# Router logits of 14 token tiles by products in four column groups, closed one step later

## The chip, the cores and the metric

The kernel runs on one core of a Trainium2 chip. The metric is the time of one execution in microseconds (us) on the device; lower is better. Engines are called by the profile's short names: PE is TensorE's matrix products, PEld its weight loads, DVE is VectorE, ACT is ScalarE, POOL is GpSimd, SP is SyncE, which only issues transfers.

## What is computed

Three layers follow each other, all in float32, on 4 x 576 = 2304 tokens of 512 features:

```python
# 1. attention, 8 heads of 64, causal window of 64
scores = scale * np.matmul(q, k.transpose(0, 1, 3, 2))
attn = softmax(where(mask, scores, -1e9))
x = np.matmul(attn, v)                      # reshaped to 2304 x 512
# 2. noisy top-2 router over 8 experts, each 512 -> 1024 -> 512
logits = x @ w_gate
noise_scale = np.log1p(np.exp(x @ w_noise))
noisy_logits = logits + noise_scale * noise
top2 = np.argpartition(-noisy_logits, 2, axis=1)[:, :2]
out[mask] += top2_w[mask, k, None] * (relu(x[mask] @ w1[e]) @ w2[e])
# 3. a dense layer 512 -> 2048 -> 512 with a gated quadratic
h = x @ w_in
out = g(h) @ w_out
```

The change is in the two products `x @ w_gate` and `x @ w_noise`, which the kernel makes together: 16 columns per token, at full float32 precision, because a wrong choice of expert would show.

## The kernel before

The tokens are cut into 18 tiles of 128. The attention stage is a software pipeline of steps u = 0, 1, 2, ... (function `step`, L674); one tile takes two steps, here called a pair, and the order of instructions on every engine is exactly the order in which the code is written. A step issues, in this order:

- on even u: the scores of the next tile (`A`, a mask product L355 and then the key products L364, each in four 64x64 quadrants of PE), and the transposes of a finished attention tile (`Ex`, L421, copied out by ACT at L423);
- the transposes of the probabilities (`C`, L387, copied out by ACT at L389);
- on even u: the row maxima of the two new score blocks on DVE (`top`, L371), each turned into a bias by POOL (L373); then on every u the exponentials of one score block on ACT (`soft`, L380, four of 128 columns);
- on odd u: the router logits of an older tile (`logits`, which calls `Gm`);
- the next pieces of routing: `place` (products of one-hot marks on PE, L632), `early`, and `advance`, which runs some DVE instructions of the generator `route(g)` and up to 2 (later 4) pairs of marks, `ohr` on DVE (L584) and `ohe` on DVE (L591) or ACT (L594);
- on even u: probabilities times values (`Dm`, L401, in two column halves of PE, all into the two banks `OB`), its division on DVE (L406 to L409) and a store of the tile to DRAM;
- two halves of splitting an expert weight into a rounded part and a remainder, ACT first and DVE behind it (`split_w`, L161 and L162).

`Gm` (L434 to L442) multiplies the transposed tile, as the stationary operand, with the 512 x 16 gate matrix: four products over 128 rows each, accumulated into 16 columns (272 to 287) of a rotating bank, which DVE copies out (L442). A float32 product appears as two records in the trace.

```python
for k in range(4):
    nc.tensor.matmul(lg, lhsT=xt[:, k, :], rhs=wg_sb[:, k, 0:2 * E], start=(k == 0), stop=(k == 3))
```

The tiles are routed in three groups of six (`tile_group`); when the logits of a group's last tile are there, `route(g)` starts. When all marks of groups 0 and 1 are placed (24 products), `early` copies the result out (L459), works out the first token numbers of expert 0 (to L475) and POOL issues three gathers of those rows (L726). Their transposes (L748) start the expert stage; the last tiles of attention and routing are finished beside it (`tail`). The stages behind, the experts and the dense layer, keep PE at work to the end. Two banks, 3 and 5 (called bank_76 and bank_77 in the order below), rotate over `Ex`, `C`, `C` and `Gm` of every pair (`rot`).

Of the kernel before, what the change touches and what calls it, by code (L numbers as in the profile page):

```python
# [11 lines left out]
F32 = mybir.dt.float32  # L12
# [5 lines left out]
AF = mybir.ActivationFunctionType  # L18
ALU = mybir.AluOpType
AX = mybir.AxisListType  # L20

P = 128
# [4 lines left out]
E, F = 8, 1024  # L27
F2 = 2048
NT = N // P
# [8 lines left out]
GROUPS = [6, 6, 6]  # L38
EARLY = 2
NA = 3  # L40
MARKS, TAIL = (2, 4), 4
Y0, LOOK = 3, 1
PTB = 3
EW, L0, LS, F0 = 7, 1, 4, 1
SC, WS, HT = 10, 4, 256
G2 = [2, 4, 4, 4, 4]
# [12 lines left out]
def fused_kernel(ctx, tc, qT, kT, v, wg, noise, wcat, out, wd=None):  # L59
    nc = tc.nc  # L60
# [18 lines left out]
    wk = rte.enter_context(tc.tile_pool(name="wk", bufs=2, side="right"))  # L79
    gp = rte.enter_context(tc.tile_pool(name="gp", bufs=2, side="right"))  # L80
    oh = rte.enter_context(tc.tile_pool(name="oh", bufs=10, side="right"))
    ac = rte.enter_context(tc.tile_pool(name="ac", bufs=1, side="right"))
# [4 lines left out]
    OB = att.enter_context(tc.tile_pool(name="pso", bufs=1, space=PS)).tile([P, 2, 512], F32, name="ob")  # L87
# [14 lines left out]
    def load_qk(j):  # L102
        q_t[j] = qbuf[:, j % 2]
        kt = k_t[j] = qk.tile([P, 4, 320], F32, tag="k", name=f"k{j}")

        for h in (slice(0, P), slice(P, 256)) if j == 0 else (slice(0, 256),):
            t = slice(256 * j + h.start, 256 * j + h.stop)
            nc.sync.dma_start(out=kt[:, :, 64 + h.start:64 + h.stop], in_=kTv[:, :, t])
            nc.sync.dma_start(out=q_t[j][:, :, h], in_=qTv[:, :, t])
        if j == 0:  # L110
            nc.vector.memset(kt[:, :, 0:64], 0.0)


    def keys_before(j):
        nc.gpsimd.tensor_copy(k_t[j][:, :, 0:64], k_t[j - 1][:, :, 256:320])
# [4 lines left out]
    def load_v(i):  # L120
        a = vp.tile([P, H * VW], F32, tag="vE", name=f"vE{i}")
        nc.sync.dma_start(out=a, in_=v[P * i:P * i + P, :])
        if i == 0:
            vO[0] = vp.tile([P, H * VW], F32, tag="vE", name="vE_")
            nc.vector.memset(vO[0][64:128, :], 0.0)
            nc.sync.dma_start(out=vO[0][0:64, :], in_=v[0:64, :])
        vE[i] = a
# [6 lines left out]
    def load_raw(n, eng=nc.sync):  # L134
        if SP <= n < NCE:

            if n % 2 == 0:
                pool["pair"] = stream((n - SP) // 2, [P, 2, 1024], F32, f"w{n}")
            whi[n] = t = pool["pair"][:, n % 2, :]
        else:  # L140
            raws[n] = t = raw.tile([P, 1024], F32, tag="raw", name=f"raw{n}")
        if NF <= n < N2:

            if n % NF == 0:
                r = E - 2 if n >= NCE else (n // NF - 1) % (E - 2)
                dyn[n // NF] = nc.values_load(cnt_i[0:1, 1 + r:2 + r], engines=[mybir.EngineType.SP], min_val=0,
                                          max_val=(E - 1) * NF)
            eng.dma_start(out=t, in_=wcat[bass.ds(dyn[n // NF] + n % NF, 1)].rearrange("o p n -> (o p) n"))
        else:
            eng.dma_start(out=t, in_=wcat[n])  # L150
# [110 lines left out]
    wg_sb = ac.tile([P, 4, 32], F32, name="wg_sb")  # L261
# [12 lines left out]
    for s in (0, 64):  # L274
        nc.gpsimd.affine_select(out=id64[s:s + 64, :], in_=id64[s:s + 64, :], compare_op=ALU.not_equal, fill=1.0,
                                base=0, pattern=[[-1, 64]], channel_multiplier=1)
        m = m0[s:s + 64]
# [13 lines left out]
    idn = cst.tile([P, P], F32, name="idn")  # L291
# [39 lines left out]
    NU = 2 * NT  # L331
# [3 lines left out]
    LGO, POS, CNT = 272, 296, 320  # L335
    turn = [0]

    def rot(u):
        turn[0] += 1
        return bank[3 + 2 * (turn[0] % 2)] if u <= NU else bank[6]  # L340
# [3 lines left out]
    pr, pts, xts, xs, lgs_g, mxs = {}, {}, {}, {}, {}, {}  # L344


    def A(i):
        j = i // 2
        qo, ko = (i % 2) * P, (i % 2) * P
        sb = [Sb[(2 * i + k) % 3] for k in range(2)]  # L350
        for k in range(2):
            r = slice(64 * k, 64 * k + 64)
            for c in range(2):
                m = masks[c][int((2 * i + c) % 9 == 0)]
                nc.tensor.matmul(sb[k][64 * c:64 * c + 64, :], lhsT=id64[r, :],  # L355
                                 rhs=m[r].unsqueeze(1).to_broadcast([64, 4, P]), start=True, stop=False)
        for g in range(4):
            for c in range(2):
                for k in range(2):
                    r = slice(64 * k, 64 * k + 64)  # L360
                    keys = k_t[j][r, g, ko + 64 * c:ko + 64 * c + P]
                    if c == 0:
                        keys = keys.rearrange("p (s n) -> p s n", s=2)[:, ::-1, :]
                    nc.tensor.matmul(sb[k][64 * c:64 * c + 64, g * P:g * P + P],  # L364
                                     lhsT=q_t[j][r, g, qo + 64 * c:qo + 64 * c + 64],
                                     rhs=keys, start=False, stop=(g == 3))
# [16 lines left out]
    def C(u):  # L383
        p = pr.pop(u)
        PTb = rot(u)
        for g in range(4):
            nc.tensor.transpose(PTb[:, g * P:g * P + P], p[:, g, :], idn)  # L387
        t = wk.tile([P, 512], F32, tag="pt", name=f"pt{u}", bufs=PTB)
        nc.scalar.activation(t, PTb, AF.Copy)  # L389
        pts[u] = t  # L390
# [37 lines left out]
    tile_group = {}  # L428
# [2 lines left out]
            tile_group[s + t] = (g, t)  # L431


    def Gm(i, u):  # L434
        g, t = tile_group[i]
        xt = xts.pop(i)
        lg = (rot(u) if u <= NU else bank[0])[:, LGO:LGO + 2 * E]
        for k in range(4):
            nc.tensor.matmul(lg, lhsT=xt[:, k, :], rhs=wg_sb[:, k, 0:2 * E], start=(k == 0), stop=(k == 3))
        if t == 0:  # L440
            lgs_g[g] = gp.tile([P, max(GROUPS), 2 * E], F32, tag="lgs", name=f"lgs{g}", bufs=3)
        nc.vector.tensor_copy(lgs_g[g][:, t, :], lg)  # L442


    state = {"C": zero8, "late": False, "first": False}
# [6 lines left out]
    def finish_ids(parts, dst=True):  # L452


        if dst:
            f1 = wk.tile([P, 512], F32, tag="pt", name="f1", bufs=PTB)
            f2 = wk.tile([P, 512], F32, tag="pt", name="f2", bufs=PTB)
        else:
# [165 lines left out]
    live, rows = [], {}  # L624
# [39 lines left out]
        soft(u)  # L664
    warm(4)

    def logits(i, u):
        Gm(i, u)
        g, t = tile_group[i]
        if t == GROUPS[g] - 1:  # L670
            live.append(route(g))
            next(live[-1])

    def step(u):  # L674
        for c in range(EW):
            if u == L0 + LS * c:
                load_raw(c)
        if u + 2 < NU:
            if (u + 2) % 4 == 0 and (u + 2) // 4 + 1 < NT // 2:
                load_qk((u + 2) // 4 + 1)  # L680
                keys_before((u + 2) // 4 + 1)
            if (u + 1) % 2 == 0 and (u + 1) // 2 + 1 < NT:
                load_v((u + 1) // 2 + 1)


        m = u // 2
        if u % 2 == 0:
            if u + 2 < NU:
                A(m + 1)
            if 0 <= m - 2 < NT:  # L690
                Ex(m - 2, u)
        if u < NU:
            C(u)
        if u % 2 == 0 and u + 2 < NU:
            top(u + 2)
            top(u + 3)
        if u + 2 < NU:
            soft(u + 2)

        if u % 2 == 1 and 0 <= m - 2 < NT:  # L700
            logits(m - 2, u)
        place()
        early()
        advance(MARKS[u > NU - 10])
        if 0 <= u - 1 < NU:
            Dm(u - 1)

        for c in range(EW):
            for h in range(2):
                if u == L0 + LS * c + 3 + h:  # L710
                    split_w(c, h)
            if u == L0 + LS * c + 4 and EW <= c + 2 < NF:
                load_raw(c + 2)
# [56 lines left out]
    pool["w7"] = w7.enter_context(tc.tile_pool(name="w7", bufs=1, reuse_waits="tile"))  # L770

    def tail():
        logits(NT - 2, NU + 1)
        Ex(NT - 1, NU + 1)
        advance(TAIL)
        yield
        logits(NT - 1, NU + 1)
        while live or oq or pq:
            place()
            advance(TAIL)  # L780
            yield
        finish_ids([(NA, NB), (0, NA), (NB, E * JB)])
        prep_gather(units[1], 0)
        count()
        rte.close()
        pool["xp"] = xpc.enter_context(tc.tile_pool(name="xp", bufs=2, reuse_waits="tile", side="right"))
        for n in range(NF, NF + 2):
            load_raw(n)
        yield
        for b in range(1, units[1]["nb"]):  # L790
            prep_gather(units[1], b)
            yield
        prep_gather(units[2], 0)

    def count():
# [26 lines left out]
        for a, src in enumerate((src_i, dst_i)):  # L822
            f = wk.tile([P, 512], F32, tag="pt", name=f"rk{a}", bufs=PTB)[:, 0:R * J * E]
            f = f.rearrange("p (r j e) -> p r j e", j=J, e=E)
# [481 lines left out]
    for s in range(len(seq)):  # L1306
        ui, n = seq[s]
        un = units[ui]
        f = n - un["ch"][0]
# [112 lines left out]
    for q, (ui, p) in enumerate(items):  # L1422
# [5 lines left out]
        while ndone < len(items) and ndone <= q + (1 if items[ndone][0] == FIRST2 else 2):  # L1428
            i = items[ndone]
# [9 lines left out]
        g = gate(*items[q + 1]) if q + 1 < len(items) and items[q + 1][0] > FIRST2 else []  # L1439
# [58 lines left out]
```

## Time and profile before

| | |
|---|---|
| median of 3 runs | 969.06 us (968.68 to 971.01) |
| the profiled execution, its own time | 969.4 us |
| its span in the trace | 967.7 us |
| span of the attention stage, to the first transposes of gathered rows | 0 to 102.8 us |
| PE busy over the span | 98% |
| DVE, ACT, POOL busy over the span | 68%, 46%, 23% |

Busy shares are means over stages with different limits. PE's records are pipelined and their ends are modelled, so a busy PE can still have waited: the distance from the start of one group of products to the start of the next is the safer reading. Idle time is named in a row by "[us <-releaser]", and "issue" is a wait for nothing that the profile shows.

### The profile page before, as it was taken

How to read it: one execution, taken by the hardware profiler on the slowest of the kernel's cores; microseconds unless marked ns; L12 is line 12 of the kernel's file. 1: busy time of each engine (PE TensorE's matmuls, PEld its weight loads, DVE VectorE, ACT ScalarE, POOL GpSimd, SP SyncE). 2: the span in 40 equal slices, each digit the busy share in tenths (PEclk: the TensorE clock that was granted, in tenths of full speed). 3: DMA queues.
4: the chain of work that ended last, by engine and by line, in shares of the span. 5: the costliest groups of instructions: out<-in, count | busy, mean ns of one | idle time of the engine just before them, and what ended most of it. 6: DMA issues, size and time to landing. Idle time of an engine off the chain costs nothing. (4 is left out here: it accounts for less than half of the span.)

```text
span 967.7 us, 18329 instructions
## 1 busy us (share of the span) xinstructions
PE 944.2 (98%) x6918; PEld 837.0 (86%) x6918; DVE 660.7 (68%) x1377; ACT 446.8 (46%) x921; POOL 218.6 (23%) x269
## 2 busy tenths in 40 slices
PE   8998899999999999999999999999999999999997
PEld 6887789998898988889888888888999899899996
DVE  4689375578997968798442366666766777677664
ACT  6887224356555555555332366344325334442221
POOL 3221113244535434344301020013002201300000
PEclk9999799999999999999999999999999999999999
DMA  8875116557877976967837357584576558556521
GB/s 249 294 236 177 56 45 204 209 195 254 285 253 261 288 250 215 298 218 238 331 118 273 119 197 244 195 302 138 175 261 213 173 174 305 174 164 209 187 95 44
DMA packets 92797, 201.17 MB, mean 208 GB/s; under 512 B 7433, under 2 KB 17929, under 8 KB 92705
## 3 DMA queue, kind: packets, MB, share of 16 engines
q1 hardware_dynamic: 85264, 177.84, 55.4%
q0 software_dynamic: 6144, 19.76, 5.7%
q10 hardware_dynamic: 1296, 2.36, 0.6%
q8 instruction: 55, 0.90, 0.4%
q14 instruction: 38, 0.30, 0.1%
HBM read 159.65 MB, written 40.29 MB: 207 GB/s over the span
## 5 line engine op out<-in xcount | busy, mean ns | idle before, releaser
L935 PE MATMUL bank<-wo,hg 128*128 128x512 f32 x864 | 238.2, 394 | 0.0
L935 PE MATMUL bank<-w,he 128*128 128x512 f32 (+3 forms) x696 | 170.5, 396 | 0.0
L935 PEld LDWEIGHTS bank<-wo,hg 128*128 128x128 f32 x864 | 147.0, 189 | 17.3
L935 PEld LDWEIGHTS bank<-w,he 128*128 128x128 f32 (+3 forms) x696 | 124.7, 184 | 26.7
L869 PE MATMUL bank<-xhie,w 128*128 128x288 f32 (+4 forms) x768 | 120.9, 299 | 1.6 <-DVE he L880 1.5
L869 PEld LDWEIGHTS bank<-xhie,w 128*128 128x128 f32 x768 | 112.0, 188 | 8.6 <-DVE he L880 3.5
L877 ACT ACTIVATE he<-bank 128x288 fp32r<-128x288 f32 (+4 forms) x96 | 40.2, 419 | 149.7 <-PE bank L869 146.1
L162 DVE TENSOR_TENSOR w<-raw,w 128x1024 fp32r<-128x1024 f32 (+1 forms) x71 | 82.0, 1154 | 32.8 <-ACT w L161 32.1
L1188 PEld LDWEIGHTS bank<-xb,wi 128*128 128x128 f32 x576 | 81.6, 191 | 12.2 <-ACT r L887 1.7
L1188 PE MATMUL bank<-xb,wi 128*128 128x256 f32 x576 | 85.9, 285 | 2.4 <-ACT r L887 1.4
L1212 ACT ACTIVATE hg<-cg 128x512 fp32r<-128x512 f32 x64 | 40.3, 629 | 100.5 <-DVE cg L1210 100.5
L1188 PEld LDWEIGHTS bank<-xc,wi 128*128 128x128 f32 x480 | 67.2, 188 | 7.6 <-DVE wg L1173 0.6
L1048 POOL TENSOR_TENSOR y<-y,y 128x512 f32<-128x512 f32 x14 | 19.1, 1362 | 228.2 <-ACT y L1047 228.2
L1188 PE MATMUL bank<-xc,wi 128*128 128x256 f32 x480 | 70.2, 281 | 0.2
L161 ACT ACTIVATE w<-raw 128x1024 fp32r<-128x1024 f32 (+1 forms) x71 | 69.3, 977 | 0.0
L869 PE MATMUL bank<-xloe,w 128*128 128x288 f32 (+4 forms) x384 | 68.1, 299 | 0.0
L880 DVE SCALAR_TENSOR_TENSOR he<-bank,he 128x320 fp32r<-128x320 f32 (+8 forms) x120 | 43.2, 399 | 34.0 <-ACT he L877 33.9
L207 POOL TENSOR_TENSOR td<-rawd 128x512 f32<-128x512 f32 x32 | 33.3, 1040 | 133.5 <-DVE rawd L205 73.7
L1206 ACT ACTIVATE mg<-cg 128x512 f32<-128x512 f32 x64 | 40.0, 626 | 48.6 <-DVE cg L1178 46.9
L1207 DVE SCALAR_TENSOR_TENSOR cg<-mg,cg 128x512 f32<-128x512 f32 x64 | 46.9, 733 | 18.8 <-ACT mg L1206 18.8
L869 PEld LDWEIGHTS bank<-xloe,w 128*128 128x128 f32 x384 | 57.4, 188 | 0.0
L1216 DVE SCALAR_TENSOR_TENSOR hg<-cg,hg 128x512 fp32r<-128x512 f32 x64 | 45.9, 717 | 9.1 <-ACT hg L1212 8.7
(301 smaller groups left out, 1587.0 us busy)
## 6 DMA issues: line engine op xcount, KB each, us to landing
wi<-w1o SPq DMA_DIRECT2D x56, 1024.0 KB, 5.5
raw<-wcat SPq DMA_DIRECT2D x64, 512.0 KB, 5.5
rawd<-wd SPq DMA_DIRECT2D x32, 512.0 KB, 5.0
w1o<-so SPq DMA_DIRECT2D x64, 256.0 KB, 5.7
y<-y_dram SPq DMA_DIRECT2D x30, 256.0 KB, 5.4
vE<-v SPq DMA_DIRECT2D x18, 260.0 KB, 4.7
x_dram<-x SPq DMA_DIRECT2D x18, 256.0 KB, 2.3
k<-kT SPq DMA_DIRECT2D x8, 512.0 KB, 6.6
```

The source lines that it names most:

```text
L161: nc.scalar.activation(w[:, 0, c], t[:, c], AF.Copy)
L162: nc.vector.tensor_tensor(out=w[:, 1, c], in0=t[:, c], in1=w[:, 0, c].bitcast(F32), op=ALU.subtract)
L207: nc.gpsimd.tensor_tensor(out=t, in0=hf, in1=lf, op=ALU.add)
L869: nc.tensor.matmul(ps, lhsT=l[k], rhs=r[:, k, s:s + w], start=(c == 0), stop=(c == len(prods) - 1))
L877: nc.scalar.activation(hh, ps, AF.Relu)
L880: nc.vector.scalar_tensor_tensor(out=t, in0=ps[:, c], scalar=0.0, in1=hh[:, c].bitcast(F32), op0=ALU.max, op1=ALU.subtract)
L935: nc.tensor.matmul(M2[b][0:w], lhsT=h2[:, o:o + w], rhs=r[n], start=(first and a == 0), stop=(last and a == end))
L1188: nc.tensor.matmul(ps, lhsT=w[:, l, k * P:k * P + P], rhs=r[:, m, k, :], start=(c == 0), stop=(c == len(prods) - 1))
L1206: nc.scalar.activation(st["m"], c, AF.Relu, scale=0.5)
L1207: nc.vector.scalar_tensor_tensor(out=c, in0=st["m"], scalar=1.0, in1=c, op0=ALU.min, op1=ALU.subtract)
L1212: nc.scalar.activation(h2[:, 0:T], c, AF.Copy, scale=-1.0)
L1216: nc.vector.scalar_tensor_tensor(out=h2[:, T:2 * T], in0=c, scalar=-1.0, in1=h2[:, 0:T].bitcast(F32), op0=ALU.mult, op1=ALU.subtract)
```

## The change

For 14 tiles (0 to 14 without 11) the stationary and the moving operand of the logit products change places. `fold` makes four products with 32 columns of the gate matrix as the stationary operand and the transposed tile as the moving one. Each writes its own 32 partitions of a bank and takes its own 32 columns of PE; they are not accumulated. The result, four partial sums below each other, is copied to SBUF as `lt` (128 x 128), by DVE for tiles 0 to 6 and by ACT for the others. One step later, on even u between `C` and `Dm`, `unfold` makes one product of `lt` with `sel`, a 128 x 16 matrix that adds the four partial sums, into columns 272 to 287 of the second bank of `OB`, which the values leave free; DVE copies the 16 columns out (`keep_logits`). Tile 11, the last of group 1, and tiles 15 to 17 stay as they were.

```diff
+FOLD = 15
...
+    folded = {}
+    sel = ac.tile([P, 2 * E], F32, name="sel")
+    nc.gpsimd.tensor_tensor(out=sel, in0=idn[:, 0:2 * E], in1=idn[:, 32:32 + 2 * E], op=ALU.add)
+    for c in (64, 96):
+        nc.gpsimd.tensor_tensor(out=sel, in0=sel, in1=idn[:, c:c + 2 * E], op=ALU.add)
+
+    def fold(i, u):
+        xt, bk = xts.pop(i), rot(u)
+        for k in range(4):
+            nc.tensor.matmul(bk[32 * k:32 * k + 32, 0:P], lhsT=wg_sb[:, k, :], rhs=xt[:, k, :], start=True, stop=True)
+        lt = wk.tile([P, P], F32, tag="lt", name=f"lt{i}")
+        if i < FOLD // 2:
+            nc.vector.tensor_copy(lt, bk[:, 0:P])
+        else:
+            nc.scalar.activation(lt, bk[:, 0:P], AF.Copy)
+        folded[i] = lt
+
+    def unfold(i):
+        lg = OB[:, 1, LGO:LGO + 2 * E]
+        nc.tensor.matmul(lg, lhsT=folded.pop(i), rhs=sel, start=True, stop=True)
+        keep_logits(i, lg)
...
+    def direct(i):
+        return i >= FOLD or tile_group[i][0] == EARLY - 1 and tile_group[i][1] == GROUPS[EARLY - 1] - 1
...
         if u % 2 == 1 and 0 <= m - 2 < NT:
-            logits(m - 2, u)
+            (Gm if direct(m - 2) else fold)(m - 2, u)
+        if u % 2 == 0 and 0 <= m - 3 < NT and not direct(m - 3):
+            unfold(m - 3)
         place()
```

How it moves instructions is shown at three places. The first is PE at the end of the stage, at tile 14 (p are probabilities, x the attention tile, ohe and ohr marks). Before:

```order
L387 MATMUL bank_77<-idn,p_1826 128x128 x4
L439 MATMUL bank_76<-wg_sb,xt_1894 128x16 x4
L632 LDWEIGHTS ohr_2_0_1919
L632 MATMUL bank_78<-ohe_2_0_1921,ohr_2_0_1919 128x145
```

and the next step of the same program:

```order
L421 MATMUL bank_77<-idn,x_1954 128x128 x4
L387 MATMUL bank_76<-idn,p_1910 128x128 x4
L632 LDWEIGHTS ohr_4_0_1978
L632 MATMUL bank_78<-ohe_4_0_1980,ohr_4_0_1978 128x145
L632 LDWEIGHTS ohr_4_1_1982
```

With the change, the same two steps:

```order
L388 MATMUL bank_77<-idn,p_1866 128x128 x4
L444 MATMUL bank_76<-xt_1935,wg_sb 32x128 x4
L662 LDWEIGHTS ohr_2_0_1962
L662 MATMUL bank_78<-ohe_2_0_1964,ohr_2_0_1962 128x145
```

```order
L422 MATMUL bank_77<-idn,x_1997 128x128 x4
L388 MATMUL bank_76<-idn,p_1951 128x128 x4
L454 MATMUL ob<-sel,lt_2016 128x16
L662 LDWEIGHTS ohr_4_0_2022
L662 MATMUL bank_78<-ohe_4_0_2024,ohr_4_0_2022 128x145
L662 LDWEIGHTS ohr_4_1_2026
```

The four logit products keep their place in the odd step, in another shape, and one product (L454) comes in on the even step, ahead of the last products of marks.

The second place is DVE where the route of group 1 begins, with the logits of tile 11 (m, t, uu, w are the first results of the route; ohr_5 and ohe_5 are the last marks of group 0). Before:

```order
L591 TENSOR_SCALAR ohe_5_1_1571<-io_179,rf_1276 128x145
L406 TENSOR_SCALAR rl_1589<-ob 128x8
L407 RECIPROCAL rl_1589<-rl_1589 128x8
L409 TENSOR_TENSOR x_1592<-ob,rl_1589 128x512
L442 COPY lgs_1048<-bank_77 128x16
L500 TENSOR_SCALAR m_1616<-lgs_1048 128x48
L503 SCALAR_TENSOR_TENSOR t_1618<-m_1616,lgs_1048 128x48
L371 TENSOR_REDUCE mx_1656<-bank_73 128x4
```

With the change:

```order
L410 TENSOR_TENSOR x_1619<-ob,rl_1616 128x512
L461 COPY lgs_1124<-bank_77 128x16
L530 TENSOR_SCALAR m_1643<-lgs_1124 128x48
L614 TENSOR_SCALAR ohr_5_0_1645<-io_179,rf_1358,tcode_184 128x128
L621 TENSOR_SCALAR ohe_5_0_1647<-io_179,rf_1358 128x145
L533 SCALAR_TENSOR_TENSOR t_1649<-m_1643,lgs_1124 128x48
L614 TENSOR_SCALAR ohr_5_1_1655<-io_179,rf_1358,tcode_184 128x128
L621 TENSOR_SCALAR ohe_5_1_1657<-io_179,rf_1358 128x145
L372 TENSOR_REDUCE mx_1691<-bank_73 128x4
```

Group 0's logits are complete one step later, so its route runs one step later throughout, and its last two pairs of marks now stand inside group 1's route, behind its first instruction.

The third place is ACT at tile 10 (p are the exponentials, w a half of a weight to split, xt the transposed tile). Before:

```order
L380 ACTIVATE p_1490<-bank_73,nb_1436 128x128 x4
L594 ACTIVATE ohe_4_0_1504<-io_179,rf_1276 128x145
L594 ACTIVATE ohe_4_1_1508<-io_179,rf_1276 128x145
L161 ACTIVATE w_1477<-raw_1241,w_1477 128x512
L423 ACTIVATE xt_1542<-bank_76 128x512
```

With the change:

```order
L381 ACTIVATE p_1514<-bank_73,nb_1458 128x128 x4
L449 ACTIVATE lt_1523<-bank_77 128x128
L162 ACTIVATE w_1501<-raw_1259 128x512
L424 ACTIVATE xt_1567<-bank_76 128x512
L390 ACTIVATE pt_1573<-bank_77 128x512
L381 ACTIVATE p_1583<-bank_74,nb_1576 128x128 x4
L624 ACTIVATE ohe_4_0_1594<-io_179,rf_1358 128x145
```

The copy `lt` stands ahead of the weight's half, and the two marks of group 0 have gone to the step behind. SP issues the same transfers in the same order, and behind the attention stage no engine's order differs.

## Rows read from the trace of the kernel before

**Rows 1.** Windows of the trace: the attention stage in three parts, its end, the start of the experts.

```profile
core 0: us, PE busy (x) PEld busy (x) DVE busy (x) ACT busy (x) POOL busy (x), PEclk, DMA share, GB/s
20.00:60.00 40.00, 39.62 (x725) 35.51 (x727) 29.79 (x92) 35.66 (x104) 10.26 (x30) 1.00 0.80 266
60.00:80.00 20.00, 18.88 (x353) 16.21 (x353) 17.18 (x55) 16.93 (x51) 3.97 (x12) 1.00 0.79 257
80.00:99.20 19.20, 16.45 (x264) 14.23 (x260) 18.09 (x80) 14.12 (x41) 3.45 (x8) 1.00 0.32 108
99.20:111.40 12.20, 7.74 (x59) 7.04 (x60) 3.73 (x11) 2.30 (x5) 2.96 (x4) 0.58 0.35 109
111.40:125.00 13.60, 13.60 (x87) 12.63 (x85) 7.06 (x38) 3.61 (x8) 0.00 (x0) 1.00 0.00 0
```

**Rows 2.** Timeline of PE over two pairs; start us, us, engine, instruction.

```profile
44.12 0.96 PE L439 MATMUL bank<-wg_sb,xt 128*128 128x16 f32 x8
45.02 0.50 PE L355 MATMUL bank<-mask,id 64*64 64x512 bf16 x4
...
48.91 0.96 PE L439 MATMUL bank<-wg_sb,xt 128*128 128x16 f32 x8
49.81 0.41 PE L355 MATMUL bank<-mask,id 64*64 64x512 bf16 x4
50.05 1.04 PE L364 MATMUL bank<-k,qbuf 64*64 64x128 f32 x32
51.02 0.65 PE L421 MATMUL bank<-idn,x 128*128 128x128 f32 x4
...
53.62 0.96 PE L439 MATMUL bank<-wg_sb,xt 128*128 128x16 f32 x8
```

**Rows 3.** Waits between 20 and 62 us: who waited for what, us in total, times, longest.

```profile
PEld bank L421 <- issue: 1.4, 8, 0.2
PEld ob L401 <- issue: 1.3, 8, 0.2
```

**Rows 4.** Timeline of ACT, the same pairs and tile 10's marks; idle time in brackets.

```profile
43.92 1.14 ACT L380 ACTIVATE p<-bank,nb 128x128 f32<-128x128 f32 x4 [0.62 <-POOL nb L373]
...
50.97 0.71 ACT L161 ACTIVATE w<-raw 128x512 fp32r<-128x512 f32 x1
...
53.42 1.14 ACT L380 ACTIVATE p<-bank,nb 128x128 f32<-128x128 f32 x4 [0.62 <-POOL nb L373]
54.43 0.62 ACT L389 ACTIVATE pt<-bank 128x512 f32<-128x512 f32 x1
...
72.09 0.80 ACT L594 ACTIVATE ohe<-io,rf 128x145 f16<-128x145 f16 x2
```

**Rows 5.** Timeline of DVE over the same stretch.

```profile
50.28 0.17 DVE L442 COPY lgs<-bank 128x16 f32<-128x16 f32 x1
...
51.72 0.69 DVE L162 TENSOR_TENSOR w<-raw,w 128x512 fp32r<-128x512 f32 x1 [0.42 <-ACT w L161]
52.33 1.28 DVE L371 TENSOR_REDUCE mx<-bank 128x4 f32<-128x512 f32 x2
```

**Rows 6.** Timeline of DVE, group 0's marks, group 1's route and the first token numbers.

```profile
73.43 0.69 DVE L162 TENSOR_TENSOR w<-raw,w 128x512 fp32r<-128x512 f32 x1 [1.17 <-ACT w L161]
...
90.99 0.31 DVE L584 TENSOR_SCALAR ohr<-io,rf,tcode 128x128 f16<-128x128 f16 x1
91.22 0.26 DVE L591 TENSOR_SCALAR ohe<-io,rf 128x145 f16<-128x145 f16 x1
91.38 1.28 DVE L371 TENSOR_REDUCE mx<-bank 128x4 f32<-128x512 f32 x2
...
96.88 0.46 DVE L459 COPY first<-bank 128x290 f32<-128x290 f32 x1 [0.32 <-PE bank L632]
```

**Rows 7.** Timeline of POOL and PE, the first gather and the transposes of what it brings.

```profile
98.43 1.21 POOL L726 DMA_INDIRECT xg0a<-x_dram,src_i  x1 [4.84 <-DVE rl L406]
```
```profile
102.78 0.75 PE L748 MATMUL bank<-idr,xg0a 128*128 128x128 f32 x4 [3.46 <-DMA xg0a<-x_dram,src_i]
```

More of the change, by code (lines that the diff above doesn't have):

```diff
@@ L431, in fused_kernel, with keep_logits @@
             tile_group[s + t] = (g, t)
+    folded = {}
[17 more added lines that the diff above has]
+        keep_logits(i, lg)
+    def keep_logits(i, lg):
+        g, t = tile_group[i]
+        if t == 0:
+            lgs_g[g] = gp.tile([P, max(GROUPS), 2 * E], F32, tag="lgs", name=f"lgs{g}", bufs=3)
+        nc.vector.tensor_copy(lgs_g[g][:, t, :], lg)
+        if t == GROUPS[g] - 1:
+            live.append(route(g))
+            next(live[-1])
     def Gm(i, u):
@@ L439, in Gm @@
             nc.tensor.matmul(lg, lhsT=xt[:, k, :], rhs=wg_sb[:, k, 0:2 * E], start=(k == 0), stop=(k == 3))
-        if t == 0:
-            lgs_g[g] = gp.tile([P, max(GROUPS), 2 * E], F32, tag="lgs", name=f"lgs{g}", bufs=3)
-        nc.vector.tensor_copy(lgs_g[g][:, t, :], lg)
+        keep_logits(i, lg)
     state = {"C": zero8, "late": False, "first": False}
@@ L665, in fused_kernel @@
     warm(4)
[L667 to L672, printed above, removed]
+    def direct(i):
+        return i >= FOLD or tile_group[i][0] == EARLY - 1 and tile_group[i][1] == GROUPS[EARLY - 1] - 1
     def step(u):
@@ L772, in tail @@
     def tail():
-        logits(NT - 2, NU + 1)
+        Gm(NT - 2, NU + 1)
         Ex(NT - 1, NU + 1)
@@ L776, in tail @@
         yield
-        logits(NT - 1, NU + 1)
+        Gm(NT - 1, NU + 1)
         while live or oq or pq:
```

## The prediction

> **What bounds the kernel now.** Read the windows first [rows 1]. Behind 111.4 us PE has no free time (13.60 of 13.60 us), and the change moves nothing there. So the question is when the expert stage can start, and that is one event: the transposes of gathered rows start at 102.78 us, when the gather lands, after PE has waited 3.46 us for it [rows 7]. The gather was issued at 98.43 us, as soon as DVE had the first token numbers; DVE reads the placed marks out at 96.88 us, 0.32 us after it ran dry, waiting for the last product of marks [rows 6]. A microsecond that the attention stage gains or loses counts only where it reaches that read-out.
>
> Now go back along the stage and ask in each part which engine sets the pace. Between 20 and 60 us PE is busy 39.62 of 40 us, which looks like a PE bound [rows 1]. The timeline of PE says otherwise: pairs last 4.79 and 4.71 us in turn (44.12 to 48.91 to 53.62), and in the longer one the mask products last 0.50 us instead of 0.41 [rows 2]: their second bank waits 0.09 us for the exponentials of an earlier score block. Follow those on ACT. The exponentials at 43.92 and at 53.42 both start at once when POOL delivers a bias, after 0.62 us idle, and they lie 9.50 us apart, exactly two pairs [rows 4]. The way between runs over ACT's weight half (50.97), the same half on DVE, which idles 0.42 us for it, then the row maxima (52.33), then POOL [rows 4, 5]. PE appears in this ring with the score products and the transposes that follow them, and the logit products do not. So two rings are about equal in length, PE's own (2 x 4.71 = 9.42 us for two pairs) and this one (9.50 us).
>
> From 80 to 99.2 us DVE is busy 18.09 of 19.20 us [rows 1]; in the timeline of DVE the only idle time named between 73.43 and 96.88 us is the 0.32 us above [rows 6]. There DVE sets the pace, with route and marks of group 1. Between 60 and 80 us DVE (17.18 of 20) and ACT (16.93) share it: DVE idles 1.17 us at 73.43 for a weight half of ACT.
>
> **PE's part of the change.** Now the logit products hold PE from 48.91 to 49.81 us, 0.90 us per tile [rows 2]. In the new shape eight records go in two sets of four. The nearest rows are the key products: 32 records in four quadrants take 0.97 us with the change of shape behind them (50.05 to 51.02), eight sets of 0.12 us at most, each streaming the same 128 columns [rows 2]. Two sets are 0.24 us. The tile shape changes once more than before; the weight loader's idle time at a change of shape is 1.4 and 1.3 us in 8 cases each, 0.17 us a time [rows 3]. That makes 0.41 us. `unfold` is one product of the old shape, a quarter of 0.90 us: 0.22 us. A tile saves 0.90 - 0.41 - 0.22 = 0.27 us of PE, 14 tiles 3.8 us. Bounds for the four products: if sets do not overlap at all, eight records of 0.12 us are 0.96 us, and a tile loses 0.45 us; if nothing is paid for the shape, it saves 0.44 us. I take the middle value, because quadrants and the two halves of the values already overlap here.
>
> What reaches the end: the other ring. Two pairs would take PE 9.42 - 0.54 = 8.88 us, and the ring over ACT, DVE and POOL still 9.50 us, so the 0.54 us turns into waiting at the mask products. What is left is a single head start, at most one pair's 0.27 us, and the second half is DVE's. I book a gain of 0.3 us; the ends are 0 and 3.8 us.
>
> **The copies.** DVE's seven copies of 128 columns lie between its copy of 16 columns (0.17 us) and 512 columns (0.69 us) [rows 5]; about 0.3 us each. They fall before 60 us, where DVE is busy 29.79 of 40 us [rows 1], and stand behind a division and ahead of the half for which DVE idles 0.42 us [rows 5]. Cost zero; without that cover, 7 x 0.3 = 2.1 us. The later copies of 16 columns are the old ones, moved. ACT's seven copies are priced by its exponentials, four of 128 columns in 1.01 us (53.42 to 54.43): 0.25 us each [rows 4], 1.75 us in all. Behind them wait, on ACT, the weight half or the transposed tile, and with the half DVE. ACT has idle time of 0.6 us or so ahead of the exponentials [rows 4], which covers some; and at tiles 8 and 10 two marks (0.80 us in the row at 72.09) have moved out of the same place. Ends 0 and 1.75 us; I take two of the seven as uncovered, 0.5 us. `sel` costs POOL three small sums before its first bias: nothing, since POOL is busy a quarter of its time from 20 to 60 us [rows 1] and the start has no bias waiting on it. SP and its transfers are unchanged.
>
> **The route of group 0, one step later.** Its work on DVE is the same, but two pairs of marks now stand behind the first instruction of group 1's route, in the stretch that DVE fills without a gap up to the gather. A pair costs 0.39 us (90.99 to 91.38) [rows 6], two 0.8 us. If DVE reaches that point earlier by as much, because the marks left a place where it was working and not idling, the cost is zero; DVE's 1.17 us at 73.43 says that it idles there for ACT, so the time freed is mostly not won. I take 0.8 us; ends 0 and 0.8.
>
> **The closing product at the end.** For tile 14 it stands on PE ahead of the last four products of marks, for which DVE waits already at 96.88 us [rows 6]. PE reaches them 0.2 us later: 0.2 us; ends 0 and 0.2.
>
> **Sum.** -0.3 + 0.5 + 0.8 + 0.2 = +1.2 us. The profiled execution took 969.4 us and would take 970.6 us; it stands 0.3 us above the median of the three runs, 969.06 us, so the forecast for a median is **970.3 us**, slower by 0.12%. About 0.3% (2.9 us) is what a measurement of this kernel can tell from no change; the three runs alone spread over 2.3 us. PE's granted clock is 0.58 between 99.2 and 111.4 us [rows 1], the lower level for most of it, behind the wait for the gather. That wait keeps its length in my sum, so I book nothing, but allow 1 us either way.
>
> **The rivals.** *PE is the bound after all* (0.10). Then the 3.8 us arrive at the gather: 969.06 - 3.8 = 965.3 us. For it speaks the 39.62 of 40 us until 60 us; against it the 0.50 us mask rows and the full DVE behind 73 us. [...]
>
> *The column groups run one after the other* (0.07). The four products stream four different operands over all 128 rows at once, which no row here shows: the quadrants stream two per row. Unoverlapped, a tile costs 0.45 us more, PE becomes the longer ring (two pairs 9.42 + 0.9 = 10.32 us against 9.50) and decides from a loss of 0.04 us a tile on. Over the eight pairs before 60 us that is 8 x 0.41 = 3.3 us, later tiles are covered by DVE, and with the other terms (1.5 us) the time is 973.9 us, slower.
>
> *Every copy of ACT is paid* (0.10): 1.75 + 0.8 + 0.2 = 2.75 us, 971.8 us. It decides where ACT, not POOL's bias, is last at the exponentials.
>
> *Nothing reaches the gather* (0.15): DVE makes up the moved marks, and the time is 969.1 us.
>
> **How the numbers follow.** The forecast as summed, 969.5 to 971.5 us, has 0.58. The range that holds 8 in 10 takes in the fourth rival, the third, and the clock's 1 us: **968.0 to 972.4 us**; the first two and the tails are left out. Faster by over 0.3% (below 966.2 us) needs most of the first rival: 0.07. Slower by over 0.3% (above 972.0 us) takes the second and part of the third: 0.11. Within 0.3%: 0.82.
>
> **What would show it.** Right: from the start of the logit products to the mask products about 0.45 us instead of 0.90, while pairs between 30 and 60 us still take 4.75 us on average and PE's mask products wait longer for ACT's exponentials; DVE without a gap from group 1's logits on; the read-out of marks and the gather about 1 us later than 96.88 and 98.43 us. Wrong: pairs of 4.5 us before 60 us with the gather before 98 us (the first rival), logit products of 0.9 us or more (the second), or a shift that arises behind 111 us.

## The result: slower by 1.2%

| | before | after |
|---|---|---|
| median (6 runs each) | 970.12 us (968.68 to 976.88) | 982.87 us (981.10 to 986.28) |
| ratio, 95% interval | | 1.0123 [1.0101, 1.0145] |
| span of the profiled execution | 967.7 us | 980.9 us |
| first gather issued | 98.43 us | 111.31 us |
| first transposes of gathered rows | 102.78 us | 115.43 us |

The forecast was 970.3 us with a range of 968.0 to 972.4. The kernel became slower by 12 us, well outside it.

Where the time went is seen first in the windows of the kernel after, over the same stretches as before [rows 1]:

```profile
core 0: us, PE busy (x) PEld busy (x) DVE busy (x) ACT busy (x) POOL busy (x), PEclk, DMA share, GB/s
20.00:60.00 40.00, 31.36 (x629) 26.19 (x627) 25.27 (x66) 31.13 (x89) 8.74 (x25) 0.98 0.72 235
60.00:80.00 20.00, 17.63 (x300) 13.56 (x296) 14.22 (x61) 14.54 (x44) 4.40 (x12) 0.86 0.61 197
80.00:99.20 19.20, 14.65 (x266) 12.57 (x267) 15.56 (x65) 14.19 (x43) 2.94 (x10) 0.92 0.58 194
99.20:111.40 12.20, 9.88 (x168) 7.74 (x167) 9.63 (x41) 8.62 (x26) 1.50 (x5) 0.98 0.20 66
```

PE's busy time between 20 and 60 us fell from 39.62 to 31.36 us, and DVE's and ACT's fell with it: no engine works in the time that PE lost. The end of the stage is the same sequence as before, shifted. POOL's first gather and PE's transposes behind it, answering to [rows 7], each in its timeline:

```profile
111.31 1.21 POOL L754 DMA_INDIRECT xg0a<-x_dram,src_i  x1 [4.46 <-DVE rl L407]
```

```profile
115.43 0.53 PE L776 MATMUL bank<-idr,xg0a 128*128 128x128 f32 x4 [3.08 <-DMA xg0a<-x_dram,src_i]
```

The gather comes 12.88 us later and the span is 13.2 us longer, so the loss is complete before the expert stage starts. Within the attention stage the twelfth pair's mask products start at 61.78 us instead of 54.52 (+7.3), the last pair's at 100.84 instead of 88.11 (+12.7).

The list of waits between 20 and 100 us (who waited for what: us, times, longest) names PE waiting for DVE ahead of the values' products, which the list of before does not have, and DVE waiting for those products 12.1 us instead of 1.6:

```profile
PEld ob L402 <- POOL nb L374: 16.0, 12, 2.6
...
DVE rl L407 <- PE ob L402: 12.1, 11, 1.3
PE ob L402 <- DVE lgs L461: 10.2, 9, 2.0
```

L402 is the values' products, L461 is DVE's copy of the 16 logits. At three more places the last entry is put down to what DVE ran just behind the copy (L547, L561, L564: 4.8 us), which makes 15.0 us of PE at twelve places. The first line is the weight loader at the same places; in the first pair shown below POOL's bias was done at 35.74 us and DVE's copy at 36.03, the loader started at 36.15, so there too the copy was last. PE's timeline over two pairs shows the place, with L454 the closing product and L444 the four column groups:

```profile
33.78 0.60 PE L388 MATMUL bank<-idn,p 128*128 128x128 f32 x4
34.21 0.29 PE L454 MATMUL ob<-sel,lt 128*128 128x16 f32 x2
36.18 1.15 PE L402 MATMUL ob<-vE,pt 128*64 128x65 f32 x32 [1.67 <-DVE lgs L461]
...
37.85 0.43 PE L444 MATMUL bank<-xt,wg_sb 128*32 128x128 f32 x8
38.21 0.41 PE L356 MATMUL bank<-mask,id 64*64 64x512 bf16 x4
...
40.35 0.29 PE L454 MATMUL ob<-sel,lt 128*128 128x16 f32 x2
41.13 1.15 PE L402 MATMUL ob<-vE,pt 128*64 128x65 f32 x32 [0.49 <-DVE lgs L461]
...
42.80 0.43 PE L444 MATMUL bank<-xt,wg_sb 128*32 128x128 f32 x8
```

and DVE's timeline of the same stretch shows why the copy is late:

```profile
34.06 0.69 DVE L163 TENSOR_TENSOR w<-raw,w 128x512 fp32r<-128x512 f32 x1 [0.89 <-ACT w L162]
34.67 1.28 DVE L372 TENSOR_REDUCE mx<-bank 128x4 f32<-128x512 f32 x2
35.87 0.16 DVE L461 COPY lgs<-ob 128x16 f32<-128x16 f32 x1
37.38 0.17 DVE L407 TENSOR_SCALAR rl<-ob 128x8 f32<-128x8 f32 x1 [1.34 <-PE ob L402]
```

The closing product is done at about 34.5 us. On DVE its copy stands behind the two row maxima, and those stand behind the weight half, for which DVE waits 0.89 us for ACT. The copy runs from 35.87 to 36.03 us, and 0.15 us later the values' products start. The wait stands ahead of the first of their 32 records. By the code of `Dm`, in which `OB[:, h // 4]` is the bank of head h, the first 16 of these records write the first bank of `OB`, which neither the closing product nor the copy touches. So the program guards `OB`, a tile of two banks, as a whole; a wait for the second bank alone would have let half of the products (about 0.5 us of their 1.09, an estimate) run ahead of it. No run tries that. Before, `C` to values was 0.53 us (46.81 to 47.34) with no closing product between:

```profile
46.81 0.60 PE L387 MATMUL bank<-idn,p 128*128 128x128 f32 x4
47.34 1.15 PE L401 MATMUL ob<-vE,pt 128*64 128x65 f32 x32
48.42 0.66 PE L387 MATMUL bank<-idn,p 128*128 128x128 f32 x4
```

Here closing product to values is 1.97 and 0.78 us in turn. From the start of the closing product's second record to the values it is 13.3 us in all over the first nine such places, up to 71 us. Pairs now take 4.95 and 6.14 us in turn (from L444 to L444: 31.71, 37.85, 42.80), 11.09 us for two, where before two took 9.50.

### The profile page after: what moved, and what is told of

It reads as the page before. It is cut to its first block, busy times and chain, and to the rows that moved or that the text cites. A ratio compares the mean times of both kernels' runs of the same rounds, so it can differ in the third digit from the quotient of the medians.

```text
span 980.9 us, 18410 instructions
## 1 busy us (share of the span) xinstructions
PE 942.4 (96%) x6946; PEld 830.6 (85%) x6946; DVE 660.8 (67%) x1384; ACT 449.1 (46%) x928; POOL 220.0 (22%) x272
## 5 line engine op out<-in xcount | busy, mean ns | idle before, releaser
L1216 PEld LDWEIGHTS bank<-xb,wi 128*128 128x128 f32 x576 | 80.4, 188 | 12.1 <-ACT r L915 1.7
```

The lines of the kernel that those rows point to most:

```text
L1216: nc.tensor.matmul(ps, lhsT=w[:, l, k * P:k * P + P], rhs=r[:, m, k, :], start=(c == 0), stop=(c == len(prods) - 1))
```

## The experiments

The theory after the traces: **the shared bank** (more exactly the tile `OB`, which holds the bank). The logits' columns are free, but the tile is not; the values' products wait until DVE has copied the logits out, and this wait is the loss. Rivals: the column groups are slow, the copies `lt` cost more than thought, the route's delay costs more than thought. Ratios are to the kernel before in the same set of runs.

| run | ratio [95%] | first gather, us |
|---|---|---|
| the change | 1.0123 [1.0101, 1.0145] | 111.31 |
| old_products_late | 1.0174 [1.0131, 1.0216] | 110.51 |
| close_in_rotating_bank | 1.0022 [1.0008, 1.0037] | 99.79 |
| close_with_next_tile | 1.0048 [1.0026, 1.0070] | 102.28 |
| half_the_tiles | 1.0095 [1.0066, 1.0125] | 107.27 |
| close_ahead_of_maxima | 1.0048 [1.0031, 1.0065] | 103.14 |
| early_group_direct | 1.0043 [1.0028, 1.0059] | 101.20 |
| all_copies_on_vector | 1.0047 [1.0029, 1.0064] | 102.48 |
| nine_tiles_direct_rest | 1.0015 [1.0001, 1.0029] | 99.03 |
| late_tiles_alone | 1.0030 [1.0017, 1.0044] | 99.58 |
| nine_tiles_half_later | 1.0007 [0.9989, 1.0024] | 95.96 |
| before_half_later | 0.9988 [0.9974, 1.0002] | 96.05 |
| all_tiles_half_later | 1.0027 [1.0011, 1.0044] | 97.84 |

The gather column is one profiled execution each (98.43 us before), so a difference of 1 us in it is not firm. From 20 to 99.2 us PE's granted clock is 1.00 in before [rows 1], but six of the profiled executions have a stretch below that: the change (its windows above), old_products_late (0.91 from 20 to 80 us), half_the_tiles (0.92 to 0.95), close_with_next_tile and late_tiles_alone (0.91 from 80 us on), and all_copies_on_vector (0.96 up to 60 us).

**The place without the column groups.** The kernel before, its old products unchanged in shape, but a step later and into the values' bank:

```diff
-        lg = (rot(u) if u <= NU else bank[0])[:, LGO:LGO + 2 * E]
+        lg = (OB[:, 1, :] if i < 15 and i != 11 else rot(u) if u <= NU else bank[0])[:, LGO:LGO + 2 * E]
...
-        if u % 2 == 1 and 0 <= m - 2 < NT:
+        if u % 2 == 1 and 0 <= m - 2 < NT and (m - 2 >= 15 or m - 2 == 11):
             logits(m - 2, u)
+        if u % 2 == 0 and 0 <= m - 3 < 15 and m - 3 != 11:
+            logits(m - 3, u)
```

> The kernel before, with its four logit products per tile in their old shape, moved for the same 14 tiles to the even step ahead of the values and written into the second bank of the values. No column groups, no lt, no copy on ACT. Theory (the values' products wait until DVE has copied the logits out of the bank they share): the wait is all there, so most of the 12.7 us comes back, 978 to 985 us, with 0.7 to 2 us between the logit products and the values in nearly every pair. Rival (the column groups, their changes of shape or their copies cost it): 969 to 972 us, no such gap. Rival (group 0's route runs a step later and crowds group 1's): 970 to 973 us.

1.0174, a little above the range expected: no column group, no `lt`, and more than the whole loss. PE's timeline has the same wait behind the old products:

```profile
47.93 0.96 PE L439 MATMUL ob<-wg_sb,xt 128*128 128x16 f32 x8
50.26 1.15 PE L401 MATMUL ob<-vE,pt 128*64 128x65 f32 x32 [1.36 <-DVE lgs L442]
```

The place alone is enough for the loss.

**The change with another bank.** One word of the change is different:

```diff
-        lg = OB[:, 1, LGO:LGO + 2 * E]
+        lg = rot(0)[:, LGO:LGO + 2 * E]
```

> The changed kernel with one line changed: the closing product goes into the next rotating bank instead of the values' bank, at the same place in the order. Theory (wait on the shared bank): the gap ahead of the values goes to 0.3 us or less, and the time to 971 to 975 us; a little stays, because the rotating bank has one user more and its copies stand in line. Rival (column groups and copies): unchanged, 981 to 985 us. Rival (route a step later): unchanged too.

1.0022: about 10 of the 12 us are gone, though the products, the copies and the route's delay are all there. PE's timeline:

```profile
41.87 0.60 PE L388 MATMUL bank<-idn,p 128*128 128x128 f32 x4
42.72 0.40 PE L454 MATMUL bank<-sel,lt 128*128 128x16 f32 x2 [0.25 <-ACT xt L424]
43.04 1.15 PE L402 MATMUL ob<-vE,pt 128*64 128x65 f32 x32
```

The values follow the closing product after 0.32 us. A smaller wait has taken the place of the large one: the rotating bank must first be free of ACT's copy `xt`.

**The copy ahead of the maxima.** The closing product stays in the values' bank, but `unfold` is called before `top`:

```diff
         if u < NU:
             C(u)
+        if u % 2 == 0 and 0 <= m - 3 < NT and not direct(m - 3):
+            unfold(m - 3)
         if u % 2 == 0 and u + 2 < NU:
             top(u + 2)
...
-        if u % 2 == 0 and 0 <= m - 3 < NT and not direct(m - 3):
-            unfold(m - 3)
         place()
```

> The changed kernel with one move: the closing product is issued a little earlier in the step, so that DVE's copy of the logits stands ahead of the two row maxima on DVE and not behind them; the bank stays the one that the values' products write. Theory A (the loss is the wait of the values' products for that copy, and its length is what stands ahead of the copy on DVE): the nine gaps between the closing product and the values' products, 14.0 us in the changed kernel, shrink to under 3 us in all; part comes back elsewhere, since the closing product now waits for the bank's earlier readers and the maxima start later. Ratio to before 1.003 to 1.008. Rival B (writing the closing product into the values' bank costs by itself, wherever the copy stands): gaps of the same sum, in front of the closing product or behind it, ratio 1.010 to 1.015.

The ratio, 1.0048, is where theory A put it. The nine gaps are 8.6 us instead of 13.3, not under 3 (counted alike, the 14.0 us of the expectation are 13.3): I had overlooked that the copy now stands right behind the weight half, and that closing product and copy take 0.62 us even when nothing is ahead of them. DVE's timeline has both parts of the order:

```profile
43.44 0.69 DVE L163 TENSOR_TENSOR w<-raw,w 128x512 fp32r<-128x512 f32 x1 [1.15 <-ACT w L162]
44.05 0.17 DVE L461 COPY lgs<-ob 128x16 f32<-128x16 f32 x1
44.13 1.28 DVE L372 TENSOR_REDUCE mx<-bank 128x4 f32<-128x512 f32 x2
```

Two pairs take 10.36 us (40.87 to 51.23 us at the mask products), between 9.50 and 11.09. So the length of the wait is what stands ahead of the copy on DVE, as the theory says.

**Half of the tiles.** `FOLD = 7`, so only tiles 0 to 6 are changed.

> The changed kernel for tiles 0 to 6 only, all lt copies on DVE; tiles 7 to 17 as before. Theory (shared bank): each tile pays its own wait, so about half of the loss, 975 to 978 us. Rival (ACT's copies, which are all gone here, or marks of group 0): 969 to 972 us.

A miss: 7 of 14 tiles cost three quarters of the loss (1.0095). Their seven gaps are 2.31, 0.76, 1.94, 0.76, 1.94, 0.75 and 2.02 us, 10.5 us, as long as in the change itself. The first tiles are the expensive ones: at the gather they cost 8.8 of the 12.9 us. I read it so that behind 60 us part of a gap falls into time in which PE waits for DVE anyway; no run shows that apart. PE's clock has a part in the 1.0095 as well: the mean granted clock of these four runs is 0.990, that of the runs of before in the same set 0.994 (more on this under "What stays open").

**The closing product a pair later**, behind the next tile's column groups and in their bank; `fold` gets the older tile as `more`:

```diff
-    def fold(i, u):
+    def fold(i, u, more=None):
...
+        lg = more is not None and unfold(more, bk)
...
+        if more is not None:
+            keep_logits(more, lg)
...
-            (Gm if direct(m - 2) else fold)(m - 2, u)
-        if u % 2 == 0 and 0 <= m - 3 < NT and not direct(m - 3):
-            unfold(m - 3)
+            (Gm if direct(m - 2) else fold)(m - 2, u, m - 3 if m > 2 and not direct(m - 3) else None)
```

> The changed kernel with the closing product a whole pair later, directly behind the next tile's four products and in their bank, copied out behind them. Theory (shared bank): no wait ahead of the values at all; what is left are ACT's copies and group 0's route, now two steps late: 970 to 975 us. Rival (column groups and their copies): 980 us or more. Rival (group 0's route): worse than the changed kernel, since it starts another step later, over 983 us.

1.0048. Here the wait ahead of the values is gone and the prediction's own sum can be read. PE's timeline over two pairs:

```profile
44.09 0.66 PE L388 MATMUL bank<-idn,p 128*128 128x128 f32 x4
44.68 0.43 PE L444 MATMUL bank<-xt,wg_sb 128*32 128x128 f32 x8
45.04 0.40 PE L457 MATMUL bank<-sel,lt 128*128 128x16 f32 x2
45.36 0.75 PE L356 MATMUL bank<-mask,id 64*64 64x512 bf16 x4
...
50.28 0.41 PE L356 MATMUL bank<-mask,id 64*64 64x512 bf16 x4
...
54.87 0.40 PE L356 MATMUL bank<-mask,id 64*64 64x512 bf16 x2
```

Pairs take 4.92 and 4.59 us, 9.51 for two: the ring of 9.50 us stands here (the two pairs ahead, 35.55 to 45.36 us, take 9.81 at the mask products, 9.51 at ACT's exponentials), and the longer of the two has the mask products spread over 0.75 us, waiting for the exponentials as the prediction had it.

The next runs start from this kernel and look for what is left of the loss. **Tile 5 direct** (`return i >= FOLD or i in (5, 11)`), so that group 0's route is not delayed:

> The kernel of the run before with the closing product behind the next tile's logit products (close_with_next_tile, 1.0048), with one more change: tile 5, the last of group 0, takes the old products, so that group 0's route starts where it did in the kernel before. Theory A (what is left of the loss in that run is the delay of the route): about 2 us of its 4.7 us go, ratio 1.001 to 1.004. Rival B (it is ACT's copies, or the later tiles' lateness of a pair): ratio stays at 1.004 to 1.006.

1.0043 against 1.0048, intervals overlapping. The gather comes 1.1 us earlier (101.20), near the 0.8 us booked for a delay of one step (here it was two), but most of the loss stays. **The same with all copies `lt` on DVE** (`if i < FOLD:`):

> As early_group_direct, with all copies of the folded products on DVE and none on ACT. Theory A (ACT's copies delay the weight halves for which DVE waits; DVE has room before 60 us only): 0 to 1.5 us below early_group_direct, ratio 0.999 to 1.003. Rival B (DVE sets the pace behind 60 us, so its copies of the later tiles, about 0.3 us each, cost more than ACT's): 0.5 to 1.5 us above early_group_direct.

1.0047: neither side is shown; which engine copies makes no difference that the runs can tell. **Column groups up to tile 8 only** (`FOLD = 9`; with tile 5 direct these are eight tiles, all copies on DVE):

> As all_copies_on_vector, with the column groups only for the tiles 0 to 8 (5 not), which lie before 60 us; the later tiles keep the old products. Theory A (up to 60 us the ring over ACT, DVE and POOL holds two pairs at 9.5 us, so that PE's saving is idle time, and all losses come later): no difference to the kernel before, ratio 0.998 to 1.002. Rival B (PE's saving does reach the gather once the wait is gone): about 0.27 us for each of eight tiles, 2 us, ratio 0.996 to 0.998.

1.0015, an interval that just leaves out 1, with the gather 0.6 us late. The other half, **tiles 9, 10, 12, 13, 14 alone** (`return i < 9 or i >= FOLD or i == 11`):

> early_group_direct with the column groups only for the tiles 9, 10, 12, 13 and 14; the tiles 0 to 8 keep the old products. Theory A (what is left of the loss once the bank is not shared comes from the tiles whose logits are made behind 60 us, where ACT and DVE set the pace and five copies of 0.25 to 0.3 us stand in their queues): 1.3 to 3 us lost, ratio 1.0015 to 1.0035. Rival B (it comes from the tiles ahead of 60 us): ratio 0.999 to 1.001.

1.0030, and the gather 1.15 us late: by the medians the tiles behind 60 us carry two thirds of what is left, though the two intervals overlap. ACT's timeline and DVE's, at tile 10, show a new wait:

```profile
71.19 1.18 ACT L381 ACTIVATE p<-bank,nb 128x128 f32<-128x128 f32 x4
72.19 0.35 ACT L450 ACTIVATE lt<-bank 128x128 f32<-128x128 f32 x1
```

```profile
70.93 0.68 DVE L163 TENSOR_TENSOR w<-raw,w 128x512 fp32r<-128x512 f32 x1
72.56 0.17 DVE L464 COPY lgs<-bank 128x16 f32<-128x16 f32 x1 [0.95 <-ACT lt L450]
```

In the kernel before, DVE's copy of 16 columns followed its weight half at once at this place:

```profile
71.05 0.68 DVE L162 TENSOR_TENSOR w<-raw,w 128x512 fp32r<-128x512 f32 x1
71.65 0.17 DVE L442 COPY lgs<-bank 128x16 f32<-128x16 f32 x1
```

DVE, which sets the pace here, idles 0.95 us until ACT has copied `lt` out of the bank in which the closing product of the older tile also stands. It is again a wait for a copy out of a shared bank, here between two readers. At tile 10 it is made up for: the second pair of mask products behind it starts at 81.21 us, 81.38 in before. At tile 14 it reaches the gather: DVE waits 0.65 us for ACT's `lt`, its copy starts at 96.30 us instead of 95.16, and the read-out of marks at 98.02 instead of 96.88. That this wait is the loss of the late tiles is not shown: the stretch also holds the lower clock (0.91), and all_copies_on_vector, in which ACT makes no `lt`, is no faster.

**DVE's weight half a step later.** If the ring of 9.50 us runs over DVE's wait for ACT's weight half, taking that wait away must shorten the pairs. `split_w` gets a `part`: ACT's half stays, DVE's is issued one step behind (the load of the next weight too):

```diff
                 if u == L0 + LS * c + 3 + h:
-                    split_w(c, h)
-            if u == L0 + LS * c + 4 and EW <= c + 2 < NF:
+                    split_w(c, h, 0)
+                if u == L0 + LS * c + 4 + h:
+                    split_w(c, h, 1)
+            if u == L0 + LS * c + 5 and EW <= c + 2 < NF:
```

In nine_tiles_direct_rest, in the kernel before, and in early_group_direct with its 13 tiles:

> nine_tiles_direct_rest with DVE's weight half issued one step behind ACT's, so that DVE does not idle for it ahead of the row maxima. Theory A (the ring over ACT's weight half, DVE's half, the row maxima and POOL's bias holds two pairs at 9.5 us, and PE's saving hides behind it): two pairs fall from 9.5 us to PE's own length, 2 x 4.59 = 9.18 us, between 25 and 55 us, and the first expert products come about 1 us earlier than in nine_tiles_direct_rest; ratio 0.998 to 1.001. Rival B (something else holds the pairs): two pairs stay at 9.5 us, ratio 1.000 to 1.003.

> The kernel before with the same delay of DVE's weight half alone. Theory A: PE's own pair of 4.71 us takes over, two pairs fall from 9.50 to 9.42 us, 0.3 us in all; ratio 0.998 to 1.001, not to be told from before, and above nine_tiles_half_later by about 0.001. Rival B: two pairs stay at 9.50 us.

> early_group_direct (column groups for tiles 0 to 14 without 5 and 11) with the same delay of DVE's weight half. Theory A: as nine_tiles_half_later before 60 us, and the loss of the tiles 9 to 14 stays, ratio 1.002 to 1.004. Rival B: no gain over early_group_direct, 1.004 to 1.005.

The ring is settled by PE's timelines, mask products alone, of the kernel with all 13 tiles and then of the kernel before, each with DVE's half later:

```profile
25.63 0.41 PE L358 MATMUL bank<-mask,id 64*64 64x512 bf16 x4
30.22 0.41 PE L358 MATMUL bank<-mask,id 64*64 64x512 bf16 x4
34.81 0.41 PE L358 MATMUL bank<-mask,id 64*64 64x512 bf16 x4
```

```profile
25.57 0.41 PE L357 MATMUL bank<-mask,id 64*64 64x512 bf16 x4
30.27 0.41 PE L357 MATMUL bank<-mask,id 64*64 64x512 bf16 x4
34.98 0.41 PE L357 MATMUL bank<-mask,id 64*64 64x512 bf16 x4
```

From 25 to 53 us every pair is now PE's own: 4.59 us with column groups (4.93 and 4.26 around the direct tile 5), 4.70 without. In nine_tiles_half_later pairs of 4.59 us stand beside one of 5.35 and that of the direct tile, 4.93. All three gathers come earlier than before, two of them by over 2 us, most of it won behind 60 us: in before_half_later PE is busy 20.00 of 20 us from 60 to 80, where before had 18.88 [rows 1]. The times don't follow as far: 1.0007, 0.9988 and 1.0027, the first two with an interval that holds 1. So none of these kernels is shown to beat the kernel before, and the column groups, expected to add 0.001 to the gain of the later half, did not.

**What stays open.** The ratios mostly lie above what the shift of the gather gives, by up to 1.8 us, by 3 us in the two kernels with column groups and the later half, and by 4.8 us in old_products_late; nine_tiles_half_later and before_half_later issue it within 0.1 us of each other, and their medians are 968.17 and 964.99 us on the same chip. In their single profiles it is behind the first transposes, where the two programs are alike, that the time differs: 867.8 and 861.2 us, at a mean granted clock of 0.993 and 0.997. The clock explains a part of it. The kernel before, in the same set, took 965.1 to 965.7 us in its runs at 0.998 and 969.6 to 969.8 us in those at 0.990, about 0.5 us for each 0.001 (an estimate). By that, the mean clocks of the twelve runs each (0.9939 and 0.9954) are worth 0.8 of the 3.2 us, and that of old_products_late (0.987 against 0.994 in before) some 3.5 of its 4.8 us. The rest stays open.

## Why the prediction was wrong, by its own steps

**The step that failed** is one clause of "The copies": "The later copies of 16 columns are the old ones, moved." I costed them at nothing, because I asked only what the copy itself takes on DVE. The new place of the copy has a waiter that the old one had not: the values' products, which write the same tile `OB`. Standing behind the weight half and two maxima, the copy makes PE wait 0.36 to 2.5 us per tile, 15.0 us at twelve places between 20 and 100 us. old_products_late shows this place alone to be enough for the loss, and close_in_rotating_bank shows 10 of the 12 us gone without it. "The closing product at the end", 0.2 us, has the same fault: it prices the product, not the wait it sets up. None of the rivals was this mechanism, and the range, built from the terms, could not hold it.

The rows for it were there. DVE idles for the weight half and then runs the maxima [rows 5], which is the queue that the copy was moved into. The change says that the closing product writes the second bank of `OB`. Neither the bank nor the tile was free in the traces. DVE's 0.95 us for ACT at 72.56 us in late_tiles_alone stands between two readers of other columns of one bank; PE's 1.67 us at 36.18 us in the change is wider, since it also holds back the products into the first bank of `OB`.

**PE's part**: the direction was right, the size was half. From the column groups to the product behind them it is 0.36 us instead of 0.90, better than the 0.41 booked. But the closing product takes 0.32 us, not 0.22, and from `C` to the logit products it grew from 0.49 us (48.42 to 48.91 [rows 2]) to 0.59 (44.09 to 44.68). A tile saves 0.90 + 0.49 - 0.59 - 0.36 - 0.32 = 0.12 us, and the two pair lengths agree, 4.59 against 4.71. From 0.90 to 0.36 us the swapped products alone are 2.5 times as fast, and 1.3 times with the closing product (0.36 + 0.32 us). The rival that the groups run one after the other is out.

**The other ring**: right. 9.51 us for two pairs from 35 to 50 us with the column groups in place, and 9.18 us (2 x 4.59) once DVE's wait for ACT's half was taken out. PE's saving was indeed idle time.

**DVE's copies `lt`**: neither the zero booked nor the 2.1 us without cover is settled. The eight tiles of nine_tiles_direct_rest, copies included, cost 0.1 to 2.8 us by the interval and 0.6 us at the gather. **ACT's copies** were priced by the distance from one start to the next, 0.25 us; by that measure they take 0.15 us (the next instruction of ACT starts at 72.34 us behind the `lt` of 72.19), though their records last 0.33 to 0.35. What the prediction did not see is that DVE waits for them at the bank (0.95 us at tile 10, 0.65 at tile 14). The five late tiles, with everything that comes with them, cost 2.9 us (1.6 to 4.3, by the ratio), against 0.5 us booked for seven copies of ACT and the rival's 1.75.

**Group 0's route**: 0.8 us booked, 1.1 us earlier at the gather without the delay; too small to tell in the times. **Behind 111 us nothing shifts**: right, +12.88 us at the gather and +13.2 us at the end.

## What to carry to other kernels

Free columns were not a free bank here (DVE waited 0.95 us for ACT's `lt`), nor a free tile (PE waited 15.0 us in all for DVE's copies out of `OB`): before a product is moved into a bank, list who else writes or reads that bank or the tile that holds it, and where the copy that frees it will stand in its engine's queue. A copy that is cheap where nobody waits for it can be the costliest instruction of a step where the bottleneck engine queues behind it: this one takes 0.16 us, and PE waited up to 2.5 us for it. Price a moved instruction by its new waiters, not by its own duration, and look for the ring that sets the pace before counting savings of an engine that shows 99% busy.

## What the runs showed of the hardware that was not expected

The four column groups of a set run together: in the changed kernel, at the clock of 1.00, their four records (L444 at 31.71 us) start within 0.02 us of each other, each streaming 128 columns of another operand, and the second set of four starts 0.13 us behind the first.

PE's granted clock fell inside the attention stage in the three profiled executions with the longest waits ahead of the values (the change, old_products_late, half_the_tiles), and in three others (named under the table of ratios). In old_products_late the windows show a stretch with 1.64 us of PE busy in 3 us, and behind it the lower clock:

```profile
36.00:39.00 3.00, 1.64 (x36) 1.55 (x36) 1.62 (x5) 1.38 (x5) 0.74 (x3) 0.95 0.97 341
39.00:42.40 3.40, 3.40 (x44) 2.55 (x43) 0.81 (x3) 1.63 (x5) 0.31 (x1) 0.54 1.02 338
42.40:46.00 3.60, 3.24 (x54) 2.90 (x55) 1.97 (x6) 2.69 (x8) 1.04 (x4) 1.00 0.09 29
```

Over the stretch with a granted clock of 0.54 the key products took 1.92 us and one pair later, at 1.00, 1.04 us (PE's timeline):

```profile
39.82 1.92 PE L364 MATMUL bank<-k,qbuf 64*64 64x128 f32 x32
...
46.03 1.04 PE L364 MATMUL bank<-k,qbuf 64*64 64x128 f32 x32
```

In the changed kernel the windows give 0.86 between 60 and 80 us and 0.92 up to 99.2, where before had 1.00 [rows 1]. Narrower windows of the changed kernel, two of them behind a wait of PE for the copy (1.76 us to 58.45, 1.30 us to 71.19), the third over one (2.5 us to 96.81):

```profile
58.00:63.00 5.00, 4.55 (x80) 3.57 (x80) 2.52 (x15) 2.84 (x10) 0.84 (x3) 0.66 0.94 322
72.00:76.50 4.50, 4.50 (x65) 3.12 (x61) 2.56 (x12) 2.53 (x8) 0.69 (x1) 0.62 0.99 334
96.00:100.00 4.00, 3.19 (x44) 2.71 (x44) 2.68 (x10) 1.20 (x5) 1.05 (x3) 0.57 0.00 1
```

Inside these the clock reads 0.50 from 59 to 62, from 73 to 75 and from 97 to 99 us; in the kernel before it reads 0.50 from 101.5 to 111 us, begun within the 3.46 us wait for the gather, and 1.00 from 111.5 us on.

A slower PE is a second price of the change. The length of each window times what its clock lacks of 1.00 is 1.7 us, so all three together cost at most 5.1 of the 12.9 us at the gather (an estimate); the part that reached the gather was not measured apart from the waits. Not every wait is followed by a fall: the changed kernel waits 1.7 us at 36.18 us and at 47.27 us as well and stays at 1.00 until 58 us, and close_ahead_of_maxima has 0.6 to 1.6 us between closing product and values at each of thirteen places and keeps 1.00 from 20 to 99.2 us.
